# Late rows gathered by two transfers, the first four output tiles stored singly, and 8 KB store runs for three batches, in an attention and spectral-mixing kernel

## The chip, the cores and the metric

The kernel runs on one core of a Trainium2 chip. The time of a run is device microseconds; the number to be compared is the median of several runs. A profiled execution gives, beside its time, the span from the first to the last instruction, every instruction with its line, and every DMA packet.

Names used below: PE is TensorE (matrix products, into PSUM), DVE is VectorE, ACT is ScalarE, POOL is GpSimd, SP is SyncE. SP and POOL each issue DMA transfers here, SP by its hardware queue (q1), POOL by its software queue (q0).

## What is computed

The reference, cut to what matters (batch B = 8, 8 heads, S = 576, head width 64, D = 512, 64 modes):

```
phi(x) = where(x > 0, x, exp(x) - 1) + 1
kv  = einsum('bhsd,bhse->bhde', phi(k), v);  z = sum_s phi(k)
x   = einsum('bhsd,bhde->bhse', phi(q), kv) / (phi(q) . z + 1e-6)     # heads side by side: (8, 576, 512)
X   = rfft(x, axis=1)[:, :64]
Y   = X @ (w_r + i w_i)          # its own 512 x 512 complex matrix for each of the 64 modes
u   = x + irfft(Y, n=576)
out = u + max(u @ w_ch, 0)       # (8, 576, 512) float32
```

The 64 modes' weights (two 512 x 512 float32 matrices each) are most of the bytes read; the output is 9.44 MB.

## The kernel before

**Stages.** Attention, the forward transform, and then one mode after the other: `w_load` (L110) brings a mode's two weight matrices in 512 KB transfers from POOL's queue, `mode_product` (L349 to L365) multiplies, and the mode's rows for all batches are collected in `YT`. Everything that the output needs and that does not depend on the last modes is worked off between the products of the modes, from a list called `work`: the attention rows, the inverse transform of modes 0 to 31 added to x (`fold`, L538), the channel product of that sum (`channel_product`, L557, kept in `E0`), and, for each batch, the rows of modes 32 to 63, as `YZ[b]`.

**YZ.** `YZ[b]` holds in [128 partitions, 2, 512] float16 the 64 rows (32 modes, real and imaginary) twice, in partitions 0 to 63 and 64 to 127, once as they are (index 0, `form_y`, L593) and once multiplied by w_ch (index 1, `form_z`, L584). When it is formed, the last NL = 8 modes are not there yet; their 16 rows (partitions 48 to 63 and 112 to 127) are filled in at the end from the tile `last`, which has the 16 rows of every batch in 128 partitions, row r of batch b in partition 8 r + b.

**The tail** starts when the last weights have landed. PE transposes the late rows (L750), ACT copies them to `last[:, 0]` (L751), PE multiplies them by w_ch in two halves of 256 columns (L757), and ACT and DVE copy a half each to `last[:, 1]` (L763, L765). Tile 0 gets its y part by a product of its own (`y0`, L767, L768). Then 14 transfers from POOL (L771) carry the late rows into the `YZ[b]`, for batches in the order 2, 3, 0, 1, 4, 5, 6, 7; the upper halves of batches 0 and 1 are not needed and left out. The tiles of batches 0 and 1 (pairs 0 to 3) do not wait for these, since they multiply by `last` itself with the selector matrices `lead_sb`.

**Output tiles and pairs.** The output goes out in 36 tiles of [128, 512] float32 (256 KB): four of each batch in `x_main[b]` and, for every two batches, one of the left-over rows in `x_tail`. `pairs` puts them in 18 pairs: 0 and 1 are batch 0, 2 and 3 batch 1, 4 and 5 batch 2, pair 6 and 8 batch 3 with 7 the first two tail tiles, 9 and 10 batch 4, 11 and 12 batch 5, 13 and 14 batch 6, 15 and 17 batch 7 with 16 the other tail tiles. For every pair, all of it pinned in program order on its engine:

- `channels(n)` (L655): PE puts the kept channel product into the pair's two PSUM banks;
- `rectified(n)` (L616, L665): PE adds the late modes' part of the channel product, and ACT takes the max with 0 in place, one tile at a time;
- `finish(n)` (L616, L695): PE adds the late modes' part of u, DVE adds x to the whole pair (128 x 1024) and writes it into x, and SP stores it (`store`, L671, 4 KB runs for two tiles that lie side by side; L677 for tail tiles, 2 KB runs). The last pair is added and stored in single tiles (L690).

PSUM holds four pairs at once. The order on PE at the start of the tail is written by hand at the end of the kernel (L781 to L799): pair 0 in single tiles, then channels(2), channels(3), rectified(2), finish(1), rectified(3), finish(2), and from pair 4 on a loop of channels(n), rectified(n), finish(n - 1). Several transfers of SP can be outstanding; the stores of a queue follow each other.

Of the kernel before, what the change touches and what calls it, by code (L numbers as in the profile page):

```python
# [10 lines left out]
F32 = mybir.dt.float32  # L11
F16 = mybir.dt.float16
BF16 = mybir.dt.bfloat16
AF = mybir.ActivationFunctionType
ALU = mybir.AluOpType
# [27 lines left out]
def kernel(  # L43
# [10 lines left out]
    nc = tc.nc  # L54

    B, H, S, Dh = q.shape
    D = H * Dh
    NM = moe_w_r.shape[0]
    NHP = H // 2
    NDC = D // 128  # L60
    NJJ = 4
# [16 lines left out]
    id16 = const.tile([128, 128], F16, name="id16")  # L78
    fwd_sb = const.tile([128, 5, 2 * NM], F16, name="fwd_sb")
    pick_sb = const.tile([128, 16], F16, name="pick_sb")  # L80
    wch16 = const.tile([128, NDC, D], F16, name="wch16")
# [41 lines left out]
    pin = tc.keep_in_program_order  # L123
# [10 lines left out]
    def rows_of(jj: int, base: int = 0):  # L134

        if jj < NJJ:
            return slice(base + jj, base + 512, NJJ)
        return slice(512, S) if base == 0 else slice(0, base)
# [274 lines left out]
    psW = tc.alloc_tile_pool(name="psW", bufs=1, space=PSUM, side="left")  # L413
# [7 lines left out]
    N_LEAD = 2  # L421
# [31 lines left out]
    sW = ctx.enter_context(tc.tile_pool(name="sW", bufs=1))  # L453
# [1 line left out]
    x_tail = [  # L455
        sW.tile([128, 2, D], F32, tag="x_tail", bufs=B // 4, name=f"x_tail{i}") for i in range(B // 4)
    ]
    YZ = [sW.tile([128, 2, D], F16, tag="YZ", bufs=B, name=f"YZ{b}") for b in range(B)]
    YE: dict[int, object] = {}
    E0: dict[int, object] = {}  # L460
    BASE = (0, 64)
# [2 lines left out]
    def x_of(t: int):  # L464
        if t < B * NJJ:
            return x_main[t // NJJ][:, t % NJJ, :]
        i = t - B * NJJ
        return x_tail[i // 2][:, i % 2, :]
# [13 lines left out]
    last_ps = []  # L482
# [7 lines left out]
    def parts_of(t: int):  # L490
        if t < B * NJJ:
            b, jj = divmod(t, NJJ)
            return [(b, jj, slice(0, 128))]
        p = t - B * NJJ
        return [(2 * p + h, NJJ, HALVES[h]) for h in range(2)]
# [76 lines left out]
    def form_z(b: int):  # L572

        z_ps = bank(f"z{b}")
        for ec in range(NDC):
            yt = YT[:, ec, NF:NM, :].rearrange("p m (t b) -> p (m t) b", b=B)[:, :, b]
            for h in range(2):
# [5 lines left out]
                )  # L583
        pin(nc.scalar.copy(out=YZ[b][:, 1, :], in_=z_ps))  # L584

    def form_y(b: int):

        y_ps = bank(f"yp{b}", [128, NDC, 128], F16)
        for ec in range(NDC):
            yt = YT[:, ec, NF:NM, :].rearrange("p m (t b) -> p (m t) b", b=B)[:, :, b]  # L590
            for h in range(2):
                pin(nc.tensor.transpose(y_ps[HALVES[h], ec, :], yt, id16))
        pin(nc.vector.tensor_copy(out=YZ[b][:, 0, :], in_=y_ps.rearrange("p c r -> p (c r)")))  # L593

    def fold_lead(t: int):
# [4 lines left out]
        sel_rows = inv2_sb[0 : 2 * NF, rows_of(jj, BASE[b % 2])]  # L600
        pin(nc.tensor.matmul(acc, sel_rows, YZ[b][0 : 2 * NF, 0, :]))
        pin(nc.vector.tensor_tensor(out=x, in0=acc, in1=x, op=ALU.add))
        e = E0[b][:, jj * D : jj * D + D]
        acc = bank(f"zb{t}")
        pin(nc.tensor.matmul(acc, id16, e, start=True, stop=False))
        pin(nc.tensor.matmul(acc, sel_rows, YZ[b][0 : 2 * NF, 1, :], start=False, stop=True))
        pin(nc.scalar.copy(out=e, in_=acc))

    last = sW.tile([128, 2, D], F16, tag="rows", bufs=1, name="last")

    def add_inverse(n: int, half: int, tiles_of=(0, 1)):

        def mm(i, orow, l, r):
            on_bank(
                n, {i},
                nc.tensor.matmul(  # L616
                    accs[n][orow, i], l, r, start=False, stop=True, skip_group_check=True
                ),
            )

        for i in tiles_of:
            for b, jj, orow in parts_of(pairs[n][i]):
                sel_rows = rows_of(jj, BASE[b % 2])
                if n < 2 * N_LEAD:
                    mm(i, orow, lead_sb[b][:, sel_rows], last[:, half, :])
                else:
                    g = HALVES[i]
                    mm(i, orow, inv2_sb[g, sel_rows], YZ[b][g, half, :])

    pairs = []  # L630
# [9 lines left out]
    def on_bank(n: int, banks: set, ins):  # L640
        pin(ins)
        for other, theirs in users.setdefault(n, []):
            if not banks & theirs:
                tc.declare_no_dep(ins.ins, other.ins, reason="the other bank of the pair")
        users[n].append((ins, banks))
    accs: dict[int, object] = {}

    def channels(n: int):
        pool = acc_pools[n % 4 // 2]
        accs[n] = pool.tile([128, 2, D], F32, tag="acc", bufs=2, name=f"acc{n}")  # L650
        for i, t in enumerate(pairs[n]):
            for cols, src in e0_parts(t):
                on_bank(
                    n, {i},
                    nc.tensor.matmul(  # L655
                        accs[n][:, i, cols], id16, src, start=(cols.start == 0), stop=False,
                        skip_group_check=True,
                    ),
                )

    def rectified(n: int):
        add_inverse(n, 1)
        for i in range(2):
            a = accs[n][:, i]
            on_bank(n, {i}, nc.scalar.activation(out=a, in_=a, func=AF.Relu))  # L665

    def store(t: int, n_t: int):
        if t < B * NJJ:
            b, jj = divmod(t, NJJ)
            r0 = b * S + BASE[b % 2]  # L670
            nc.sync.dma_start(  # L671
                out=out_rows[r0 : r0 + 512, :].rearrange("(r j) d -> r j d", j=NJJ)[:, jj : jj + n_t, :],
                in_=x_main[b][:, jj : jj + n_t, :],
            )
            return
        i = t - B * NJJ
        nc.sync.dma_start(  # L677
            out=out_rows.rearrange("(i r) d -> r i d", i=B // 2)[512:640, i : i + 2, :],
            in_=x_tail[i // 2],
        )  # L680

    def finish(n: int):
        acc = accs[n]
        single = n == len(pairs) - 1
        t0 = pairs[n][0]
        add_inverse(n, 0)
        for i, t in enumerate(pairs[n]):
            if single:
                x = x_of(t)
                on_bank(n, {i}, nc.vector.tensor_tensor(out=x, in0=acc[:, i], in1=x, op=ALU.add))  # L690
                store(t, 1)
        if single:
            return
        x = x_main[t0 // NJJ][:, t0 % NJJ : t0 % NJJ + 2, :] if t0 < B * NJJ else x_tail[(t0 - B * NJJ) // 2]
        on_bank(n, {0, 1}, nc.vector.tensor_tensor(out=x, in0=acc, in1=x, op=ALU.add))  # L695
        store(t0, 2)

    def spread(n_items: int, step: int, steps: int):
# [43 lines left out]
                work.append(lambda n=n: channels(n))  # L742


    last_ps.append(psW.tile([128, D], F32, tag="P", bufs=2, name="zl1"))
    y_ps = psW.tile([128, NDC, 128], F16, tag="P", bufs=2, name="ypl")
    y0_ps = psW.tile([128, NDC, 8, 2 * B], F32, tag="yt", bufs=1, name="y0l")
    rows = [YT[:, ec, NE:NM, :].rearrange("p m n -> p (m n)") for ec in range(NDC)]
    for ec in range(NDC):
        pin(nc.tensor.transpose(y_ps[:, ec, :], rows[ec], id16))  # L750
    pin(nc.scalar.copy(out=last[:, 0, :], in_=y_ps.rearrange("p c r -> p (c r)")))  # L751
    hw = D // 2
    for h in range(2):
        cols = slice(h * hw, h * hw + hw)
        for ec in range(NDC):
            pin(
                nc.tensor.matmul(  # L757
                    last_ps[h][:, 0:hw], rows[ec], wch16[:, ec, cols],
                    start=(ec == 0), stop=(ec == NDC - 1),
                )  # L760
            )
        if h == 0:
            pin(nc.scalar.copy(out=last[:, 1, cols], in_=last_ps[h][:, 0:hw]))  # L763
        else:
            pin(nc.vector.tensor_copy(out=last[:, 1, cols], in_=last_ps[h][:, 0:hw]))  # L765
    y0 = y0_ps.rearrange("p c m n -> p (c m n)")
    pin(nc.tensor.matmul(y0, lead_sb[0][:, rows_of(0)], last[:, 0, :]))  # L767
    pin(nc.vector.tensor_tensor(out=x_of(0), in0=y0, in1=x_of(0), op=ALU.add))  # L768
    for b in (2, 3, 0, 1, 4, 5, 6, 7):
        for h in range(1 if b < N_LEAD else 2):  # L770
            nc.gpsimd.dma_start(out=YZ[b][64 * h + 48 : 64 * h + 64, :, :], in_=last[b::B, :, :])  # L771
    psW.release()
    acc_pools.append(
        tc.alloc_tile_pool(name="psT1", bufs=1, space=PSUM, side="left", reuse_waits="tile")
# [2 lines left out]
    def relu(n: int, i: int):  # L777
        a = accs[n][:, i]
        on_bank(n, {i}, nc.scalar.activation(out=a, in_=a, func=AF.Relu))

    add_inverse(0, 1)  # L781
    on_bank(
# [2 lines left out]
            out=x_of(0), in0=accs[0][:, 0], scalar=0.0, in1=x_of(0), op0=ALU.max, op1=ALU.add  # L785
        ),
    )
    store(0, 1)
    relu(0, 1)
    rectified(1)  # L790
    channels(2)
    add_inverse(0, 0, (1,))
    on_bank(0, {1}, nc.vector.tensor_tensor(out=x_of(1), in0=accs[0][:, 1], in1=x_of(1), op=ALU.add))
    store(1, 1)
    channels(3)
    rectified(2)
    finish(1)
    rectified(3)
    finish(2)  # L799
    for n in range(4, len(pairs)):  # L800
        channels(n)
        rectified(n)
        finish(n - 1)
# [32 lines left out]
```

## Time and profile before

| What | us |
|---|---|
| median of 4 runs (lowest, highest) | 429.46 (429.01, 430.01) |
| the profiled execution | 429.1 |
| its span, first to last instruction | 427.3 |
| PE busy | 283.9 (66% of the span) |
| DVE busy | 212.3 (50%) |
| ACT busy | 153.5 (36%) |
| POOL busy | 95.6 (22%) |
| software queue (q0): 82.26 MB | 99.0% of the engines' span |
| hardware queue (q1): 9.78 MB | 6.0% |

How to read the views that follow. In the 40 slices each digit is the busy share of a fortieth of the span in tenths, and the GB/s row is what the DMA engines moved in it. The chain of waits gives, for each piece, its start and length in us, the engine, the tile and the line. In the stretches a line has the stretch, its length, then the busy time of PE, PE's weight loads, DVE, ACT and POOL with the number of instructions, then the granted clock of PE, the share of the DMA engines and their GB/s. A row of DMA issues has the transfer, the queue, the number, KB of each, and the median us from issue to landing. A row of DMA queues has packets, MB, and the share of the 16 engines.

### The profile page before, as it was taken

To read this page: it belongs to the slowest core of one execution; us is meant where nothing else is said; L and a number is where in the kernel's file an instruction comes from. 1 tells how busy PE (TensorE), PEld (TensorE's weight loads), DVE (VectorE), ACT (ScalarE), POOL (GpSimd) and SP (SyncE) were. 2 spreads that over 40 slices of the span, in tenths; PEclk is the share of its full clock that TensorE was granted. 3 is DMA by queue.
4 is the path that set the end of the run, shared out by engine and by line. 5 is a ranking of instruction groups with operands and counts; after the bars stand their busy time and mean duration, and the time that the engine had idled before them with its cause. 6 is when DMAs were issued, how large, how long until landed. Compare 5 with 4: busy or idle time off the path is not lost.

```text
span 427.3 us, 6617 instructions
## 1 busy us (share of the span) xinstructions
PE 283.9 (66%) x2692; PEld 158.6 (37%) x2692; DVE 212.3 (50%) x432; ACT 153.5 (36%) x240; POOL 95.6 (22%) x173
## 2 busy tenths in 40 slices
PE   0358777787119665655333797877788778997991
PEld 0346555564004433333111333433334334573320
DVE  1699998956003755556100433434353344421892
ACT  3687666631102100000000244434344343430791
POOL 4232223212201322122122122121121112010600
PEclk9996666656557655555555569899898899999996
DMA  8999999999999999999999999999999999996697
GB/s 150 207 208 209 209 210 209 212 214 212 220 211 214 214 214 213 215 212 214 214 214 212 213 214 214 213 214 213 214 214 212 214 214 214 213 214 133 221 406 301
DMA packets 35854, 92.46 MB, mean 216 GB/s; under 512 B 3216, under 2 KB 16400, under 8 KB 35824
## 3 DMA queue, kind: packets, MB, share of 16 engines
q0 software_dynamic: 32256, 82.26, 99.0%
q1 hardware_dynamic: 3568, 9.78, 6.0%
q8 instruction: 21, 0.34, 0.3%
q14 instruction: 9, 0.07, 0.0%
HBM read 163.93 MB, written 9.44 MB: 406 GB/s over the span
## 4 chain that ended last, share of the span: by engine, by line
DMA 77%; PE 8%; DVE 6%; issue 5%; POOL 1%; ACT 1%; DVEq 0%; POOLq 0%
DMA wi<-in_moe_w_i_dram 61%; DMA wr<-in_moe_w_r_dram 4%; DMA pick_sb<-row_pick 4%; DMA q<-in_q_dram 4%; DMA k<-in_k_dram 3%; PE acc L616 3%; PE P L349 2%; DVE x L267 2%; PE acc L655 2%; DVE qe L195 1%; ACT ke L182 1%; DVE q L189 1%; DVE rd L264 0%; ACT qT L218 0%; DVE k L189 0%
## 5 line engine op out<-in xcount | busy, mean ns | idle before, releaser
L349 PE MATMUL P<-wi,xt_c 128*32 128x512 bf16 x252 | 37.4, 530 | 42.4 <-DMA wi<-in_moe_w_i_dram 42.4
L360 ACT CAST ys<-P 128x512 f16<-128x512 f32 x31 | 18.1, 585 | 125.9 <-PE P L349 125.9
L110 POOL DMA_DIRECT2D wr<-in_moe_w_r_dram x64 | 34.0, 531 | 123.1 <-PE P L349 101.2
L110 POOL DMA_DIRECT2D wi<-in_moe_w_i_dram x65 | 34.5, 531 | 117.2 <-PE P L349 89.3
L358 DVE CAST ys<-P 128x512 f16<-128x512 f32 x32 | 22.1, 690 | 72.7 <-PE P L349 72.7
L349 PEld LDWEIGHTS <-xt_c 128*32 128x32 bf16 x504 | 28.6, 155 | 77.2 <-issue 65.9
L349 PE MATMUL P<-wr,xt_c 128*32 128x512 bf16 x252 | 37.8, 539 | 21.2 <-DMA wr<-in_moe_w_r_dram 19.3
L557 PE MATMUL eps<-wch,xTw 128*128 128x512 f16 x144 | 42.1, 421 | 0.0
L538 DVE TENSOR_TENSOR x_main<-ya,x_main 128x512 f32<-128x512 f32 x32 | 22.1, 691 | 40.0 <-PE ya L534 39.9
L146 PEld LDWEIGHTS <-qT 64*128 64x128 f16 (+1 forms) x640 | 23.5, 126 | 41.4 <-issue 21.3
L365 PE MATMUL yt<-pick_sb,ys 128*128 128x16 f16 x252 | 16.5, 175 | 25.4 <-DMA pick_sb<-row_pick 15.1
L540 ACT CAST x16w<-x_main 128x512 f16<-128x512 f32 x32 | 19.8, 618 | 34.5 <-DVE x_main L538 34.5
L565 ACT CAST E<-eps 128x512 f16<-128x512 f32 (+1 forms) x40 | 21.3, 543 | 27.0 <-PE eps L557 27.0
L146 PE MATMUL num<-kv,qT 64*128 64x65 f16 (+1 forms) x320 | 13.6, 225 | 22.9 <-ACT kv L242 19.5
L365 PEld LDWEIGHTS <-ys 128*128 128x128 f16 x252 | 12.1, 102 | 40.6 <-issue 17.8
L182 ACT ACTIVATE qe<-q 128x1152 f16<-128x1152 f16 x16 | 17.7, 1156 | 22.8 <-DMA q<-in_q_dram 22.8
L211 PE MATMUL qTp<-id,qe 128*128 128x128 f16 x144 | 16.7, 311 | 11.8 <-DVE qe L195 11.4
L267 DVE TENSOR_TENSOR x<-num,rd 128x512 f16<-128x512 f32 x32 | 22.1, 692 | 1.1
L146 PE MATMUL nw<-kv,qT 64*128 64x65 f16 (+1 forms) x320 | 19.6, 236 | 1.1 <-DVE x_tail L508 0.9
L182 ACT ACTIVATE ke<-k 128x1152 f16<-128x1152 f16 x16 | 17.7, 1155 | 4.9 <-DMA k<-in_k_dram 4.9
L211 PEld LDWEIGHTS <-qe 128*128 128x128 f16 x144 | 14.7, 147 | 12.6 <-DVE qe L195 11.4
L665 ACT ACTIVATE acc<-acc 128x512 f32<-128x512 f32 x34 | 18.1, 581 | 2.3 <-PE acc L616 1.7
(101 smaller groups left out, 449.4 us busy)
## 6 DMA issues: line engine op xcount, KB each, us to landing
wr<-in_moe_w_r_dram POOLq DMA_DIRECT2D x64, 512.0 KB, 18.7
wi<-in_moe_w_i_dram POOLq DMA_DIRECT2D x63, 512.0 KB, 18.9
out_dram<-x_main SPq DMA_DIRECT2D x14, 512.0 KB, 5.8
q<-in_q_dram POOLq DMA_DIRECT2D x8, 576.0 KB, 13.3
k<-in_k_dram POOLq DMA_DIRECT2D x8, 576.0 KB, 14.4
v<-in_v_dram POOLq DMA_DIRECT2D x8, 576.0 KB, 16.6
out_dram<-x_main SPq DMA_DIRECT2D x4, 256.0 KB, 3.7
out_dram<-x_tail SPq DMA_DIRECT2D x2, 512.0 KB, 6.2
```

Source lines behind the costliest of these rows:

```text
L110: tc.keep_in_program_order(nc.gpsimd.dma_start(out=w[:, dcs], in_=rows_of[:, dcs, :]))
L146: mm = nc.tensor.matmul(num[hpo][orow, c0 : c0 + 65], qT[rows, hpp, h2, cols], kv_sb[rows, hpp, h2, :])
L182: pin(nc.scalar.activation(out=ev[:, c], in_=heads(nm, b)[:, c], func=AF.Exp))
L211: nc.tensor.transpose(qT_ps[:, j].rearrange("p t r -> p (t r)"), phi["q", b][:, hpp, j].rearrange("p o d -> p (o d)"), id16,)
L267: nc.vector.tensor_tensor(out=dst.rearrange("p (o c d) -> p o c d", o=2, c=4), in0=nv[:, :, :, 0:64], in1=rden.unsqueeze(3).broadcast_to([ ...
L349: nc.tensor.matmul(P[dc * 32 : dc * 32 + 32, :], xt_cols(dc, t, kk), w[:, dc, :], start=(t == 1), stop=(t == 0), tile_position=(0, dc * 32),)
L358: fixed(nc.vector.tensor_copy(out=st, in_=P))
L365: nc.tensor.matmul(yt_ps[:, ec, kk % 8, :], st[:, ec * 128 : ec * 128 + 128], pick_sb)
L538: pin(nc.vector.tensor_tensor(out=x, in0=acc, in1=x, op=ALU.add))
L540: pin(nc.scalar.copy(out=x16w[t], in_=x))
L557: nc.tensor.matmul(e_ps, xT[:, c, :], wch16[:, c, :], start=(c == 0), stop=(c == NDC - 1))
L565: pin(nc.scalar.copy(out=dst, in_=e_ps[:, cols]))
```

## The change

- `YZ` becomes one tile `YZ_all` [128, 8, 2, 512], of which `YZ[b]` is a slice.
- The 14 gathers become two, one for each half of the partitions, 16 partitions x 8 batches x 2 KB each; the lower half is issued by SP, ahead of the first store, the upper half by POOL.
- The transposed late rows go through two PSUM tiles, one copied by ACT and one by DVE; both halves of the product by w_ch are copied by ACT. The PSUM tiles of this stage change places (`z1` takes the slot of `y0`, and `y0` one of the two slots of the transposes).
- Pair 1 is finished in two single tiles, as pair 0 is, and on PE `channels(3)` moves from ahead of `rectified(2)` to behind pair 1.
- For batches 4, 5 and 6 a pair's add issues no store of its own; the second pair's add issues one store of all four tiles (1 MB, 8 KB runs in the output).

```
-    YZ = [sW.tile([128, 2, D], F16, tag="YZ", bufs=B, name=f"YZ{b}") for b in range(B)]
+    YZ_all = sW.tile([128, B, 2, D], F16, tag="YZ", bufs=1, name="YZ_all")
+    YZ = [YZ_all[:, b] for b in range(B)]
...
+    QUADS = (4, 5, 6)
...
         on_bank(n, {0, 1}, nc.vector.tensor_tensor(out=x, in0=acc, in1=x, op=ALU.add))
+        if t0 < B * NJJ and t0 // NJJ in QUADS:
+            if t0 % NJJ:
+                store(t0 - 2, NJJ)
+            return
         store(t0, 2)
...
-    last_ps.append(psW.tile([128, D], F32, tag="P", bufs=2, name="zl1"))
-    y_ps = psW.tile([128, NDC, 128], F16, tag="P", bufs=2, name="ypl")
-    y0_ps = psW.tile([128, NDC, 8, 2 * B], F32, tag="yt", bufs=1, name="y0l")
+    z1_ps = psW.tile([128, NDC, 8, 2 * B], F32, tag="yt", bufs=1, name="z1l")
+    y_ps = [
+        psW.tile([128, NDC, 128], F16, tag="P", bufs=2, name=f"ypl{h}")[:, 0 : NDC // 2] for h in range(2)
+    ]
+    y0 = psW.tile([128, D], F32, tag="P", bufs=2, name="y0l")
+    last_ps.append(z1_ps.rearrange("p c m n -> p (c m n)"))
...
-        pin(nc.tensor.transpose(y_ps[:, ec, :], rows[ec], id16))
-    pin(nc.scalar.copy(out=last[:, 0, :], in_=y_ps.rearrange("p c r -> p (c r)")))
+        pin(nc.tensor.transpose(y_ps[ec // 2][:, ec % 2, :], rows[ec], id16))
+    pin(nc.scalar.copy(out=last[:, 0, COLS[0]], in_=y_ps[0].rearrange("p c r -> p (c r)")))
+    pin(nc.vector.tensor_copy(out=last[:, 0, COLS[1]], in_=y_ps[1].rearrange("p c r -> p (c r)")))
...
-        if h == 0:
-            pin(nc.scalar.copy(out=last[:, 1, cols], in_=last_ps[h][:, 0:hw]))
-        else:
-            pin(nc.vector.tensor_copy(out=last[:, 1, cols], in_=last_ps[h][:, 0:hw]))
+        pin(nc.scalar.copy(out=last[:, 1, COLS[h]], in_=last_ps[h][:, 0:hw]))
...
-    for b in (2, 3, 0, 1, 4, 5, 6, 7):
-        for h in range(1 if b < N_LEAD else 2):
-            nc.gpsimd.dma_start(out=YZ[b][64 * h + 48 : 64 * h + 64, :, :], in_=last[b::B, :, :])
+    for h, eng in enumerate((nc.sync, nc.gpsimd)):
+        eng.dma_start(
+            out=YZ_all[64 * h + 48 : 64 * h + 64].rearrange("r b z d -> r b (z d)"),
+            in_=last.rearrange("p z d -> p (z d)"),
+        )
...
+    def add_one(n: int, i: int):
+        t = pairs[n][i]
+        on_bank(n, {i}, nc.vector.tensor_tensor(out=x_of(t), in0=accs[n][:, i], in1=x_of(t), op=ALU.add))
+        store(t, 1)
...
     channels(2)
     add_inverse(0, 0, (1,))
-    on_bank(0, {1}, nc.vector.tensor_tensor(out=x_of(1), in0=accs[0][:, 1], in1=x_of(1), op=ALU.add))
-    store(1, 1)
+    add_one(0, 1)
+    rectified(2)
+    for i in range(2):
+        add_inverse(1, 0, (i,))
+        add_one(1, i)
     channels(3)
-    rectified(2)
-    finish(1)
     rectified(3)
     finish(2)
```

More of the change, by code (lines that the diff above doesn't have):

```diff
@@ L742 @@
                 work.append(lambda n=n: channels(n))
-    last_ps.append(psW.tile([128, D], F32, tag="P", bufs=2, name="zl1"))
-    y_ps = psW.tile([128, NDC, 128], F16, tag="P", bufs=2, name="ypl")
-    y0_ps = psW.tile([128, NDC, 8, 2 * B], F32, tag="yt", bufs=1, name="y0l")
+    z1_ps = psW.tile([128, NDC, 8, 2 * B], F32, tag="yt", bufs=1, name="z1l")
[4 more added lines that the diff above has]
+    last_ps.append(z1_ps.rearrange("p c m n -> p (c m n)"))
     rows = [YT[:, ec, NE:NM, :].rearrange("p m n -> p (m n)") for ec in range(NDC)]
+    hw = D // 2
+    COLS = [slice(h * hw, h * hw + hw) for h in range(2)]
     for ec in range(NDC):
-        pin(nc.tensor.transpose(y_ps[:, ec, :], rows[ec], id16))
-    pin(nc.scalar.copy(out=last[:, 0, :], in_=y_ps.rearrange("p c r -> p (c r)")))
-    hw = D // 2
+        pin(nc.tensor.transpose(y_ps[ec // 2][:, ec % 2, :], rows[ec], id16))
+    pin(nc.scalar.copy(out=last[:, 0, COLS[0]], in_=y_ps[0].rearrange("p c r -> p (c r)")))
+    pin(nc.vector.tensor_copy(out=last[:, 0, COLS[1]], in_=y_ps[1].rearrange("p c r -> p (c r)")))
     for h in range(2):
-        cols = slice(h * hw, h * hw + hw)
         for ec in range(NDC):
@@ L757 @@
                 nc.tensor.matmul(
-                    last_ps[h][:, 0:hw], rows[ec], wch16[:, ec, cols],
+                    last_ps[h][:, 0:hw], rows[ec], wch16[:, ec, COLS[h]],
                     start=(ec == 0), stop=(ec == NDC - 1),
@@ L761 @@
             )
-        if h == 0:
-            pin(nc.scalar.copy(out=last[:, 1, cols], in_=last_ps[h][:, 0:hw]))
-        else:
-            pin(nc.vector.tensor_copy(out=last[:, 1, cols], in_=last_ps[h][:, 0:hw]))
-    y0 = y0_ps.rearrange("p c m n -> p (c m n)")
+        pin(nc.scalar.copy(out=last[:, 1, COLS[h]], in_=last_ps[h][:, 0:hw]))
     pin(nc.tensor.matmul(y0, lead_sb[0][:, rows_of(0)], last[:, 0, :]))
     pin(nc.vector.tensor_tensor(out=x_of(0), in0=y0, in1=x_of(0), op=ALU.add))
-    for b in (2, 3, 0, 1, 4, 5, 6, 7):
-        for h in range(1 if b < N_LEAD else 2):
-            nc.gpsimd.dma_start(out=YZ[b][64 * h + 48 : 64 * h + 64, :, :], in_=last[b::B, :, :])
+    for h, eng in enumerate((nc.sync, nc.gpsimd)):
[3 more added lines that the diff above has]
+        )
     psW.release()
```

## The prediction

> **What bounds the kernel now.** I read the 40 slices of the page first, then the chain of waits of the last 33 us, then busy time and DMA by stretches, then the DMA issues and the timelines of SP, POOL, PE and DVE.
>
> ```profile
> PE   0358777787119665655333797877788778997991
> DVE  1699998956003755556100433434353344421892
> DMA  8999999999999999999999999999999999996697
> GB/s 150 207 208 209 209 210 209 212 214 212 220 211 214 214 214 213 215 212 214 214 214 212 213 214 214 213 214 213 214 214 212 214 214 214 213 214 133 221 406 301
> ```
>
> Up to slice 36 the DMA engines are full with the weights and no compute engine is. The change leaves that stage alone, but for where the rows of YZ lie. It acts in the last four slices: the last weight lands, the transfers stop, and the output (9.44 MB) has to go out. The chain of waits of this tail, after the last mode:
>
> ```profile
> 394.47 0.40 PE ypl L750 x4
> 394.87 0.89 PE zl L757 x8
> 395.78 0.43 DVE last L765
> 396.26 1.05 PE acc L616 x4
> ...
> 417.27 1.23 DVE x_tail L695
> 418.50 0.60 DVEq L831
> 419.09 0.60 DVE x_main L690
> ```
>
> It names PE and DVE, but ends with the add at 419.7, and the span lasts to 427.3. The 7.6 us behind it are stores still on their way. So I take the transfers themselves by stretches (last two columns: share of the DMA engines, GB/s):
>
> ```profile
> 398.50:400.00 1.50, 1.50 (x8) 0.74 (x7) 0.90 (x2) 1.32 (x4) 1.50 (x4) 1.00 0.89 313
> 400.00:401.50 1.50, 1.50 (x8) 0.55 (x7) 1.50 (x2) 1.25 (x3) 1.50 (x4) 1.00 0.61 205
> 401.50:403.00 1.50, 1.50 (x11) 0.27 (x8) 1.50 (x3) 1.24 (x4) 1.50 (x5) 1.00 0.95 343
> 403.00:404.50 1.50, 1.50 (x13) 0.56 (x12) 1.50 (x2) 1.48 (x3) 0.47 (x1) 1.00 0.97 346
> 404.50:406.00 1.50, 1.50 (x14) 0.48 (x10) 1.47 (x2) 1.11 (x4) 0.00 (x0) 1.00 0.95 341
> 406.00:422.00 16.00, 11.89 (x66) 2.92 (x63) 13.47 (x13) 10.68 (x20) 0.00 (x0) 0.92 1.02 405
> 422.00:424.00 2.00, 0.00 (x0) 0.00 (x0) 0.00 (x0) 0.00 (x0) 0.00 (x0) 0.50 1.03 389
> ```
>
> From 406 to 424 the engines are full at 405 GB/s (389 in 2 KB runs). The store stream sets the end, DVE runs ahead of it (one pair of tiles, 524 KB, in 1.13 to 1.25 us of DVE and 1.29 us of DMA), and SP's issues stretch from 0.33 us at 400.56 to 1.91 at 411.16. **What counts is how many store bytes are out by 406.** Up to there the stream is poor: it moved 1.5 x (313+205+343+346+341) = 2322 KB where 405 GB/s would be 3037, and part of that was gathers:
>
> ```profile
> YZ<-last POOLq DMA_DIRECT2D x14, 32.0 KB, 2.8
> ```
>
> POOL issues them from 396.78 to 403.47. Two stream before 398.5 (a window from 397.8 to 398.45 shows 0.06 MB of the software queue); 12 x 32 KB = 384 KB come later. Stores out by 406: 2322 - 384 = 1938 KB.
>
> **The change, part by part.** *The late rows.* The second half of z is copied by ACT (L763 row: 0.38) and no longer by DVE (L765: 0.42), ready at 396.16 for 396.20; ACT is idle there until 396.97, so this costs nothing. The y copy is halved between ACT and DVE; neither is late, as the y0 product (395.58) waits for PE's eight z products in front of it anyway. DVE loses L765, so the y0 add moves from 396.12 to about 396.0. I give the tail 0.1 us from this (bounds 0.05 and 0.2).
>
> *Tiles 2 and 3 singly.* Before, the pair add starts at 399.31 after 0.60 us of waiting for PE, and its store is issued at 400.56. Now channels(3) (two products of 0.22 on PE) stands behind, so rectified(2) runs at 397.8 and the product for tile 2 at 398.2; ACT's relu of it is done at 398.04. DVE adds tile 2 when tile 1 is done: 398.6 to 399.3, tile 3 to 400.0 (0.69 each; two cost 1.38 for 1.23). Stores at 399.3 and 400.0, half a pair 1.2 us and the other half 0.5 us earlier. PE then has channels(3), rectified(3) and finish(2), six products of 0.22 from 398.9: the add of pair 2 starts at 400.3 (was 400.45), its store is issued at 401.55 (was 401.69). So this part moves two tiles only; behind them DVE's own pace rules, 0.13 us ahead.
>
> *Fourteen gathers become two*, of 256 KB each (512 KB, as the unused upper halves of batches 0 and 1 go along). POOL loses 6.69 us of issuing, and nobody but the gathers waited for POOL. SP issues one at about 396.2, ahead of store(0) on its queue; SP is idle until 397.63. POOL's goes out at about 396.7 (it needed 0.58 us after the data before, too). With the 0.87 us that store(0) takes from issue (397.63) to stream (398.50), the first flows at 397.1, with POOL's 1.0 us (issue 396.78, first bytes about 397.85) the second at 397.8: in the empty stretch ahead of the stores. The trace shows no such transfer. Bounds: at the stream's 405 GB/s 0.65 us each; the slowest burst that I find where gathers lie back to back is
>
> ```profile
> q0 software_dynamic: 96, 0.10, 43.3%
> ```
>
> in the window 400.3 to 401.0, 98 KB in about 0.66 us, or 149 GB/s: 1.76 us each. I take 1.1. Landing takes 0.5 to 1.1 us more (the 32 KB ones land 1.8 at least, 2.8 median, after issue). So both are in the rows between 399.1 and 401.7; taken: 400.2.
>
> The wait that this adds: rectified(4) on PE reads both transfers' rows (every batch under one count), where before it needed only the first two gathers. PE reaches it at 400.5. Behind it on PE stand the two products of finish(3), for which DVE waits, and then a store. Pair 3's bytes are due when pair 2's are out (402.4 + 1.29); with 0.87 of issue, 1.2 of adding and 0.9 of PE work this allows a landing up to about 400.65. Later than that costs one for one.
>
> [...]
>
> *What the stream then does.* Tiles 0 to 3 (1049 KB) flow from 398.4, each as its store comes, until 401.5; pair 2 starts at 402.4. From there the supply holds; at the share that the stretches from 401.5 show (0.96), 3.6 us x 405 x 0.96 = 1400 KB by 406. Stores out by 406: 2449 KB, 511 more than before: **1.26 us**.
>
> *8 KB runs* for batches 4 to 6 (3.15 MB). Per packet, 2 KB at 389 GB/s is 84 ns and 4 KB at 405 is 162, so a packet carries some 6 ns of its own; 8 KB would be 413 GB/s: a gain of 0.16 us, or 0 if the runs are cut at 4 KB. Taken: 0.08. Against it, the first pair of a batch waits 1.15 us for the second. Pairs 2 to 8 are out at 411.6; batch 4's store is issued at 411.0 and flows at 411.9: 0.3 us dry for most engines. But one engine has the window's instruction fetch to carry ("q8 instruction: 1, 0.02, 0.5%" from 410 to 423, 1.0 us on one of 16), ends last and is never dry. Taken: 0.1 (bounds 0 and 0.4). Tiles 2 and 3 in 2 KB runs: 0.05.
>
> Sum: -1.26 - 0.08 + 0.1 + 0.05 = -1.2 us. The profiled execution took 429.1 (span 427.3 and 1.8 around it), so 427.9; it lies 0.36 under the median of the runs, 429.46, so on that scale **428.3**.
>
> **Rivals.** *B, the gain is eaten by the gathers (no change).* All bytes of both go to the same engines in series, store(0) queues behind the first on SP's ring, and both run at 149 GB/s: 397.1 + 2 x 1.76 = 400.6, in the rows at 401.7, pair 3 1.05 us late, and the four singles shoved to 403.3. For it: 16 rows only, and large. Against: the halves go to different partitions, and most of the gathers' packets show no longer time than the stores'. Gain 0.1 to 0.2: 429.3.
>
> *C, slower.* The same wait at rectified(4), with a landing beyond 400.65 + 1.26 = 401.9; that is where two transfers in series run under 137 GB/s. The farthest row is the fourteen gathers' own mean, 448 KB in 6.69 us, 67 GB/s (set by POOL's issuing): 3.9 us each, landing at 405.9, 4 us slower on balance. At two thirds of the burst's rate, 100 GB/s, it would be 403.3 and 1.4 us slower: 430.9. For it: one count for all batches, so the batch needed first waits for the last. Against: the burst.
>
> *D, the change does not do what it says*: YZ as one tile makes copies and products of the form stage (L584, L593, L601) wait for each other, or SP issues store(0) first. The first is hidden by the weights (the chain there is 18.7 us pieces of wi), and x_main's halves are already added and stored without waits within one tile. Price about the whole gain: 429.4.
>
> **How the numbers follow.** About 0.2% (0.86 us) is what a measurement can tell from no change. Forecast 0.60, of which 0.52 faster (under 428.6) and 0.08 within; B 0.22 (0.04 faster, 0.16 within, 0.02 slower); C 0.14, all slower; D 0.04 within. Faster 0.56, within 0.28, slower 0.16. The forecast's own range is 427.6 to 428.9 (gathers at 0.65 us each, nothing dry, up to a landing of 401.2). Reaching over B and the near part of C: 427.6 to 430.2.
>
> **What would show it.** Right: two gathers that flow before 399.5; four 256 KB stores with the fourth issued near 400.0; no wait for a transfer at L616; share 0.9 or more from 402.4 on; the last add of DVE barely earlier, the last landing 1.2 us earlier. Wrong: PE idle in front of rectified(4) until after 400.7 with DVE idle behind it (B, C); a share under 0.9 near 411.6 (the 8 KB stores); any wait by L584 or L593 that grows between 358 and 383 (D).

## The result, and the profile after

The changed kernel takes 430.2 us (median of 43 runs, 429.03 to 432.17) where the kernel before takes 429.24 (64 runs): **0.21% slower, ratio 1.0021, 95% interval 1.0012 to 1.003**. The forecast was 1.2 us faster. Its profiled execution took 430.15 us, with a span of 428.4.

The two executions differ by 1.05 us, which falls in two parts. I count the tail from the end of DVE's copy of the last mode's rows (L402): 394.41 before, 394.95 after. From there to the end of the span it is 32.92 us before and 33.42 after, **0.5 us longer**. The other 0.54 us lies ahead of the tail, and the last part of this text comes back to it.

In the chain of waits of the changed kernel's tail (start, length, what) a transfer stands where before only PE and DVE stood:

```profile
396.98 5.99 DMA YZ_all<-last
402.97 0.04 issue
403.01 0.93 PE acc L617 x3
```

POOL's gather is issued at 396.98 and lands at 402.97. The DMA issues between 396.5 and 403.2 (number, KB of each, us to landing):

```profile
out_dram<-x_main SPq DMA_DIRECT2D x4, 256.0 KB, 4.9
out_dram<-x_main SPq DMA_DIRECT2D x1, 512.0 KB, 4.6
YZ_all<-last SPq DMA_DIRECT2D x1, 256.0 KB, 5.4
YZ_all<-last POOLq DMA_DIRECT2D x1, 256.0 KB, 6.0
```

A 32 KB gather had taken 2.8 us. These take 5.4 and 6.0, and the single stores beside them 4.9 where the first one before took 2.5. PE in program order, with the wait in brackets:

```profile
400.54 0.59 PE L656 MATMUL acc<-E,id 128*128 128x512 f16 x2
402.18 0.37 PE L617 MATMUL acc<-YZ_all,inv_sb 64*128 64x512 f16 x1 [1.04 <-DMA YZ_all<-last]
403.01 0.37 PE L617 MATMUL acc<-YZ_all,inv_sb 64*128 64x512 f16 x1 [0.47 <-DMA YZ_all<-last]
```

These are channels(4) and the two products of rectified(4): the lower tile waits for SP's gather, the upper one for POOL's. The products of finish(3) stand behind them, and DVE waits for those:

```profile
403.98 2.36 DVE L698 TENSOR_TENSOR x_main<-acc,x_main 128x1024 f32<-128x1024 f32 x2 [2.02 <-PE acc L617]
```

The stretches (last two columns: share of the DMA engines, GB/s):

```profile
398.50:400.00 1.50, 1.50 (x8) 0.73 (x7) 1.50 (x3) 1.46 (x3) 0.00 (x0) 1.00 1.13 187
400.00:401.50 1.50, 1.14 (x6) 0.43 (x5) 1.16 (x2) 1.07 (x2) 0.00 (x0) 1.00 1.01 134
401.50:403.00 1.50, 0.37 (x1) 0.11 (x1) 0.47 (x1) 0.41 (x1) 0.00 (x0) 1.00 0.98 280
403.00:404.50 1.50, 1.49 (x7) 0.49 (x8) 0.52 (x1) 0.75 (x2) 0.00 (x0) 1.00 1.07 412
404.50:406.00 1.50, 1.50 (x10) 0.26 (x6) 1.50 (x2) 1.23 (x3) 0.00 (x0) 1.00 0.80 326
...
413.00:415.00 2.00, 2.00 (x12) 0.37 (x8) 2.00 (x3) 1.74 (x5) 0.00 (x0) 1.00 0.78 305
```

The first two lines are the ones to learn from. The DMA engines are *full* (share 1.13 and 1.01) and move 187 and 134 GB/s, against 405 where they carry stores: they are held, not idle. At 404.5 they are short of work (0.80), since DVE is 2 us late. At 413 they are short again (0.78): the first 1 MB store, of batch 4, is issued at 413.56 and its first packet runs at 414.40.

### The profile page after: what moved, and what is told of

Read it like the earlier page. It is cut to its first block, busy times and chain, and to the rows that moved or that the text cites. A ratio compares the mean times of both kernels' runs of the same rounds, so it can differ in the third digit from the quotient of the medians.

```text
span 428.4 us, 6605 instructions
## 1 busy us (share of the span) xinstructions
PE 283.8 (66%) x2692; PEld 159.0 (37%) x2692; DVE 212.7 (50%) x433; ACT 153.9 (36%) x241; POOL 89.3 (21%) x160
## 4 chain that ended last, share of the span: by engine, by line
DMA 74%; PE 11%; DVE 6%; issue 5%; POOL 1%; ACT 1%; DVEq 0%; POOLq 0%
DMA wi<-in_moe_w_i_dram 61%; DMA pick_sb<-row_pick 4%; DMA q<-in_q_dram 4%; DMA k<-in_k_dram 3%; PE P L349 3%; PE acc L617 2%; DVE x L267 2%; PE acc L656 1%; DMA YZ_all<-last 1%; PE z L580 1%; PE zb L607 1%; PE zb L606 1%; PE yb L602 1%; DVE qe L195 1%; ACT ke L182 1%
```

## The experiments

The theory (L): the two large gathers land too late, PE's products for pair 4 wait for them, and the stores behind run late; without that, the change gains. Rivals: Q, the 1 MB stores starve the stream; D, YZ as one tile makes the form stage wait.

All results first. Times are us from the copy L402 of each profiled execution; the ratio is that of the runs to the kernel before on the same chip.

| kernel | large gathers landed | PE waits at pair 4 | last store landed | ratio (95%) |
|---|---|---|---|---|
| before | (14 small) | 0 | 31.93 | 1 |
| changed | 7.18, 8.02 | 1.51 | 32.38 | 1.0021 (1.0012 to 1.003) |
| after14 | (14 small) | 0 | 31.09 | 0.9994 (0.9982 to 1.0007) |
| two_only | 6.33, 8.31 | 1.61 | 32.53 | 1.0040 (1.0027 to 1.0052) |
| noquad | 6.84, 8.24 | 1.73 | 32.76 | 1.0032 (1.002 to 1.0044) |
| h0_only | 6.02 | 0 | 30.52 | single run |
| yz_tile | (14 small) | 0 | 32.08 | 0.9997 (0.9987 to 1.0007) |
| best14 | (14 small) | 0 | 31.04 | 0.9989 (0.9976 to 1.0002) |
| mix14 | (14 small) | 0 | 31.44 | 0.9987 (0.997 to 1.0004) |
| singles | (14 small) | 0 | 31.72 | 0.9995 (0.9973 to 1.0017) |
| quad_only | (14 small) | 0 | 31.55 | 0.9995 (0.9977 to 1.0014) |
| one_half | (8 small) | 0 | 34.00 | 1.0061 (1.004 to 1.0083) |
| spread_rows | 4.98, 5.89 | 0 | 30.38 | **0.9966 (0.9953 to 0.998)** |
| pool_both | 6.28, 8.34 | 1.69 | 32.71 | single run |

**after14: the change with the old gathers.**

```
-    for h, eng in enumerate((nc.sync, nc.gpsimd)):
-        eng.dma_start(out=YZ_all[64 * h + 48 : 64 * h + 64]..., in_=last...)
+    for b in (2, 3, 0, 1, 4, 5, 6, 7):
+        for h in range(1 if b < N_LEAD else 2):
+            nc.gpsimd.dma_start(out=YZ[b][64 * h + 48 : 64 * h + 64, :, :], in_=last[b::B, :, :])
```

> The changed kernel with the fourteen gathers of before from POOL; all else of the change kept. Theory L (late landing: the two large gathers landed at 402.1 and 403.0, PE stood 1.0 and 0.5 us in front of rectified(4), DVE 2.0 us behind it): with small gathers the wait goes, DVE has no gap over 0.4 us between 399 and 405, and the kernel is 0.6 to 1.4 us faster than the changed one, so 0.2% to no change against before (ratio 0.998 to 1.000; the gathers again lie beside the stores, which takes back most of the 1.26 us that was forecast). Rival Q (the loss comes from the 1 MB stores of batches 4 to 6 and not from the landing): DVE's gap goes, but the time stays within 0.3 us of the changed kernel, ratio 1.001 to 1.003.

The wait is gone, the tail is 1.2 us shorter than the changed kernel's, and the ratio falls from 1.0021 to 0.9994, a time that can't be told from before. Its stretches, from 3.6 us after the copy (same columns):

```profile
397.70:399.20 1.50, 1.50 (x8) 0.73 (x7) 1.50 (x3) 1.44 (x3) 1.50 (x4) 1.00 0.73 239
399.20:400.70 1.50, 1.50 (x9) 0.54 (x7) 1.16 (x2) 1.08 (x3) 1.50 (x4) 1.00 0.87 286
400.70:402.20 1.50, 1.50 (x9) 0.45 (x9) 1.40 (x2) 1.24 (x3) 1.50 (x4) 1.00 0.96 329
```

No stretch here is held as the changed kernel's were. Theory L passes, Q fails: the 1 MB stores are still in this kernel.

**two_only: the large gathers alone, in the kernel before** (YZ as one tile, the two transfers of the change, nothing else).

> The kernel before with the two large gathers (and YZ as one tile) alone; order of the tail, copies of the late rows and stores as before. Theory L: both land 5 to 6 us after issue, near 402 to 403, PE waits 1.5 to 2.4 us at the product for pair 4 that it reached at 400.6, and the kernel is 0.6 to 1.6 us slower than before, ratio 1.0015 to 1.004. Rival Q: the gathers alone cost nothing or gain, ratio 0.997 to 1.000.

1.7 us slower by the ratio. PE:

```profile
401.13 0.37 PE L617 MATMUL acc<-YZ_all,inv_sb 64*128 64x512 f16 x1
403.12 0.37 PE L617 MATMUL acc<-YZ_all,inv_sb 64*128 64x512 f16 x1 [1.61 <-DMA YZ_all<-last]
```

The lower gather is just in time here (it landed 4.5 us after issue, earlier than the 5 to 6 expected), the upper one 1.6 us late. By the medians this edit alone costs more than the whole change, so that the other edits would give part of it back; the two intervals overlap, so this is likely and not shown.

**noquad: the change with two-tile stores** (`QUADS = ()`).

> The changed kernel with two-tile stores for batches 4 to 6, as before. In the changed kernel the store stream runs at 0.53 to 0.75 of the DMA engines from 413.5 to 415, after batch 4's first pair waited for its second. If that costs the end: 0.3 to 0.5 us faster than the changed kernel, ratio to before 1.000 to 1.0015. If the late landing alone counts: within 0.2 us of the changed kernel, ratio 1.0015 to 1.003. Under rival Q alone: back at before or better, ratio 0.997 to 1.000.

Slower than the change, if anything, so the short share at 413 in the changed kernel is not where the time goes. The shortage itself did go,

```profile
413.00:415.00 2.00, 2.00 (x12) 0.48 (x12) 2.00 (x3) 1.85 (x4) 0.00 (x0) 1.00 0.99 389
```

but my expectation that this would save 0.3 to 0.5 us was wrong: the last store lands 0.4 us later than the change's (32.76 for 32.38), the second gather 0.2 later. Why the time gained did not show is open.

**quad_only: the 1 MB stores alone, in the kernel before.**

> The kernel before with the 1 MB stores for batches 4 to 6 alone. If 8 KB runs are really cheaper per byte (8 KB packets took 300 to 330 ns in the changed kernel, two of 4 KB 325): 0 to 0.3 us faster, ratio 0.9993 to 1.000. If the stream runs dry while the second pair is awaited: a stretch under 0.9 of the DMA engines near 411 to 414 and ratio 1.000 to 1.001.

Between 1.0 us faster and 0.6 slower by the interval, so not settled by time; in the profile the stream never runs dry (0.98 or more in each microsecond from 410 to 416) and carries more:

```profile
405.00:411.00 6.00, 6.00 (x33) 1.41 (x32) 5.91 (x6) 5.36 (x11) 0.00 (x0) 1.00 1.02 404
...
413.00:420.00 7.00, 4.72 (x28) 1.35 (x26) 6.39 (x7) 4.28 (x8) 0.00 (x0) 1.00 1.01 413
```

404 GB/s with mostly 4 KB runs, 413 with mostly 8 KB.

**singles: the early single tiles alone, in the kernel before.**

> The kernel before with tiles 2 and 3 added and stored singly and channels(3) behind them on PE; gathers, copies of the late rows and stores of later batches as before. If the early tiles give what the prediction gave them apart from the gathers (two tiles 0.5 to 1.2 us earlier, the rest 0.13 us): 0.2 to 0.5 us faster, ratio 0.999 to 0.9995. If DVE's extra 0.15 us counts more: 1.000 to 1.0005.

Tiles 2 and 3 are stored 4.97 and 5.57 us after the copy (the pair: 6.15) and the last store lands 0.2 us earlier. The ratio is 0.9995 with too wide an interval to say more.

**yz_tile: only YZ as one tile, in the kernel before.**

> The kernel before with YZ as one tile of eight slices and nothing else changed. Rival D of the prediction (one tile makes the copies and products of the form stage wait for each other): waits of ACT and DVE between 355 and 384 grow, the last weights land later, ratio 1.001 to 1.002. Against it: no change, ratio 0.999 to 1.001.

No change. The waits of the form stage (engine, line, what it waited for: us, times, longest) are, with one tile,

```profile
DVE YZ_all L594 <- PE yp L593: 10.2, 7, 2.0
```

and the same to the digit in the kernel before:

```profile
DVE YZ L593 <- PE yp L592: 10.2, 7, 2.0
```

ACT's (8.4 us, 8 times, longest 1.6) are the same in both, too. D falls.

**h0_only: SP's gather alone; the upper halves' late rows are left out.**

> The changed kernel with SP's gather (lower partitions) alone; the upper halves of the late rows are left out. It shows how long one such transfer takes by itself. If the two transfers share one limit (together 512 KB in 4.95 us, 106 GB/s, from the first packet at 398.02 to the second landing at 402.97), it lands 3.9 to 4.6 us after issue (5.4 with both). If each has a limit of its own, it lands at 5.2 to 5.6 as before. If bytes alone count, as for a 256 KB store (2.5), it lands at 2.5 to 3.2. PE's wait at rectified(4) shrinks by as much as the landing comes earlier.

```profile
YZ_all<-last SPq DMA_DIRECT2D x1, 256.0 KB, 4.3
```

4.3 us alone and 5.4 with its twin; no wait at PE. So the two delay each other, but even one is far over the 2.5 of a 256 KB store.

**micro: transfers of 256 KB one at a time.** Zeros are stored as the output; then each transfer waits for the one before.

> Not the kernel's computation: zeros are stored as the output and then transfers of 256 KB inside SBUF run one at a time, two rounds, 2 KB runs, from 128 partitions to: 16 neighbouring partitions (d16), 32 (d32), 64 (d64), 128 (d128), 16 partitions eight apart (dstep), all from SP; 16 from POOL (dpool); SP and POOL together into the lower and upper 16 (dlo, dhi) and into the same 16 (dlo, dsame); eight of 32 KB from POOL (dsmall). If what counts is how few places of SBUF the destination reaches: d16 3.8 to 4.5 us from issue to landing, d128 2.2 to 2.8, d32 and dstep between them. [...] If bytes alone count: all 2.2 to 2.8. For the pair: if the engines work off one transfer after the other, dlo and dhi land as late as dlo and dsame (the second 6 to 6.5 us after issue); if the two halves of SBUF take data side by side, dlo and dhi are clearly earlier than dlo and dsame.

(The profile leaves the numbers out of names: `d` is d16, d32, d64 and d128.)

```profile
d<-src SPq DMA_DIRECT2D x8, 256.0 KB, 3.9
dlo<-src SPq DMA_DIRECT2D x4, 256.0 KB, 4.5
dstep<-src SPq DMA_DIRECT2D x2, 256.0 KB, 3.0
dpool<-src POOLq DMA_DIRECT2D x2, 256.0 KB, 4.1
dhi<-src POOLq DMA_DIRECT2D x2, 256.0 KB, 6.1
dsame<-src POOLq DMA_DIRECT2D x2, 256.0 KB, 6.3
```

In the second round d16, d32, d64 and d128 took 4.1, 3.9, 3.9 and 2.3. The bytes and the runs are the same, so the place decides. Much of the difference lies behind the packets: d16's run for 1.6 us, from 1.2 to 2.8 after issue, and it lands 1.3 us later; d128's run for 0.8 and it lands 0.3 later. Of the pair, the second lands at 6.1 into the other half of SBUF and at 6.3 into the same 16 partitions: going to the other half gains 0.2 us, and they are 2.0 and 2.2 us behind the 4.1 of one alone.

**micro_spread: the same with other places.**

> As the earlier run of transfers one at a time (zeros as output, not the kernel's computation), 256 KB from SP each, now to: 16 neighbouring partitions (dnext), 16 four apart within the lower half (dfour), 16 eight apart over both halves (deight), 32 neighbours across the middle (dacross, 48 to 79), 32 four apart (dboth), 64 across the middle (dmid, 32 to 95), every second partition (dtwo), all (dall); then 16 four apart in the upper half (dupper), and dfour and dupper together from SP and POOL. Before: 16, 32 and 64 neighbours in the lower half 4.1, 3.9 and 3.9 us, 16 eight apart 3.0, 128 2.3. If the half of SBUF is the limit: dfour 3.9 to 4.1, all that reach both halves 2.2 to 3.1. If neighbours are the limit: dfour near 3.0, dacross near 4.0.

```profile
dfour<-src SPq DMA_DIRECT2D x4, 256.0 KB, 3.1
dnext<-src SPq DMA_DIRECT2D x2, 256.0 KB, 4.4
deight<-src SPq DMA_DIRECT2D x2, 256.0 KB, 3.0
dacross<-src SPq DMA_DIRECT2D x2, 256.0 KB, 3.9
dboth<-src SPq DMA_DIRECT2D x2, 256.0 KB, 2.3
dmid<-src SPq DMA_DIRECT2D x2, 256.0 KB, 2.8
dtwo<-src SPq DMA_DIRECT2D x2, 256.0 KB, 2.4
dall<-src SPq DMA_DIRECT2D x2, 256.0 KB, 2.3
dupper<-src SPq DMA_DIRECT2D x2, 256.0 KB, 3.0
dupper<-src POOLq DMA_DIRECT2D x2, 256.0 KB, 3.9
```

Sixteen partitions four apart take 3.0 in one half alone, where sixteen neighbours took 4.1, and 32 neighbours across the middle are as slow (3.9) as within a half: here the neighbourhood counts and not the half. But 64 neighbours take 2.8 across the middle (dmid) and took 3.9 within one half (d64), so the half counts too, and neither alone orders all the rows. The pair of spread transfers (dfour and dupper's POOL row) lands at 3.1 and 3.9, where the neighbours landed at 4.5 and 6.1. (dnext's median holds a first transfer behind the zero stores, 4.6; the other took 4.1.)

**spread_rows: the change with the late rows at every fourth partition.** The order of YZ's rows is free as long as the selector has the same one. The rows of modes 32 to 55 are kept in a tile `Y2` whose every fourth place stays empty, the last modes in `YL`; the transfers have the same number, bytes and runs, and the same work is computed.

```
-        ...tensor_copy(out=sel[:, 0, h * 64 : h * 64 + 64], in_=id16[:, 2 * NF : 128])
+        ...tensor_copy(out=sel[:, 0, h * 64 : h * 64 + 64].rearrange("p (s c) -> p s c", c=4),
+                       in_=id16[:, 2 * NF : 128].rearrange("p (c s) -> p s c", c=4))
...
+    Y2 = ystage.tile([128, NDC, 16, 4, B], F16, name="Y2")
...
-            out=YZ_all[64 * h + 48 : 64 * h + 64].rearrange("r b z d -> r b (z d)"),
+            out=YZ_all[64 * h + 3 : 64 * h + 64 : 4].rearrange("r b z d -> r b (z d)"),
```

> The changed kernel with the late rows at every fourth partition of each half of YZ (3, 7, ... 63 and 67 ... 127) and no longer at 48 to 63 and 112 to 127; the rows of the selector and of the early modes change places with them, so the same is computed, by the same two transfers of the same bytes. If neighbouring destination partitions are what made the transfers late: they land 3.1 to 3.5 us (SP) and 3.8 to 4.5 us (POOL) after issue where it was 5.4 and 6.0, PE's wait in front of rectified(4) falls from 1.5 us to under 0.5, and the gain that the prediction looked for appears: last landing 0.8 to 1.6 us earlier than before (counted from the copy of the last mode's rows), ratio 0.996 to 0.999. If the length of the transfers or their running in series beside the stores is the cause: landing and time as in the changed kernel, ratio 1.001 to 1.004.

```profile
out_dram<-x_main SPq DMA_DIRECT2D x4, 256.0 KB, 3.1
out_dram<-x_main SPq DMA_DIRECT2D x1, 512.0 KB, 2.8
YZ_all<-last SPq DMA_DIRECT2D x1, 256.0 KB, 3.2
YZ_all<-last POOLq DMA_DIRECT2D x1, 256.0 KB, 3.9
```

3.2 and 3.9 us to landing, as in the run by itself; single stores 3.1 for 4.9; no wait at PE. POOL's 64 data packets took 202 ns each on average, 480 in the changed kernel. The stretches (the copy ends at 395.01, so they can be laid on those of the changed kernel):

```profile
398.50:400.00 1.50, 1.50 (x8) 0.69 (x7) 1.48 (x3) 1.50 (x4) 0.00 (x0) 1.00 1.06 315
400.00:401.50 1.50, 1.50 (x9) 0.53 (x8) 1.16 (x2) 1.08 (x3) 0.00 (x0) 1.00 0.98 337
401.50:403.00 1.50, 1.50 (x10) 0.45 (x8) 1.39 (x2) 1.18 (x3) 0.00 (x0) 1.00 0.95 361
```

315, 337 and 361 GB/s for 187, 134 and 280. The kernel is **1.5 us faster than before** (ratio 0.9966) and beats both kernels. Nothing of the change was taken away, only the place of the rows. The edit also keeps the rows in other tiles ahead of the tail, but the gain is in the tail itself, counted from the copy: 31.42 us for 33.42. So the place was the cause.

**pool_both: both large gathers from POOL**, so that none stands ahead of the stores on SP's queue.

> The changed kernel with both large gathers issued by POOL, so that none stands ahead of the stores on SP's ring. If the first store's delay (landed 5.4 us after issue, 2.5 before) comes from standing behind the gather on the same ring: it lands 2.5 to 3.5 us after issue, while the second gather lands about 0.5 us later than the 8.0 of the changed kernel (from the copy of the last rows). If the engines themselves are held by the gathers, the first store still takes 4 us or more.

The first store, with no gather ahead of it on its queue now, still lands 5.4 us after issue (3.10 to 8.53 after the copy), and the second gather 0.3 us later than in the change. From 398.8 to 401.6 the DMA engines move 149 GB/s on average here too. The engines are held, not the queue.

**best14, mix14, one_half: other ways to get the rows there.** best14 is after14 with eight YZ tiles; mix14 issues the lower gathers of batches 2, 3 and 4 from SP; one_half sends only the eight lower gathers and reads the lower copy for both tiles (`g = HALVES[0]`).

> The changed kernel with the fourteen gathers and the eight YZ tiles of before; the single tiles, the copies of the late rows and the 1 MB stores of the change stay. The same tail as with one tile and fourteen gathers (last landing 0.84 us earlier than before, counted from the copy of the last mode's rows): ratio 0.997 to 0.9995, and within 0.1% of the run with one tile if the tile does nothing, 0.1 to 0.2% better if rival D holds.

> As the one before, with the lower gathers of batches 2, 3 and 4 issued by SP ahead of its first store (0.35 us each) and the other eleven by POOL. Three gathers less lie beside the stores and POOL is done 1.4 us earlier: last landing 0.1 to 0.4 us earlier than with all from POOL, ratio 0.996 to 0.999. If SP's three push the first store back by more than they save: within 0.1% of it or slower.

> The run with fourteen gathers and eight YZ tiles, but only the eight lower gathers: both tiles of a pair multiply by the lower copy of the rows, so 192 KB less lie beside the stores. The DMA engines get 0.4 to 0.6 us back. Against it, two products of 64 rows can't run side by side on PE any more (0.33 us for two, 0.43 one after the other): some 0.2 us more for a pair of tiles, 1.3 to 1.4 us for each, where the store stream needs 1.29. If the stream still sets the end: ratio 0.997 to 0.999; if PE becomes the bound: DVE gets gaps of 0.1 to 0.2 us in front of each pair and the ratio is 1.000 to 1.005.

best14 and mix14 lie between 0.3% faster and no change. mix14's earlier gathers were expected to land the last store 0.1 to 0.4 us earlier than best14's; it landed 0.4 later in the one profile, and the ratios do not differ. In one_half PE becomes the bound, as its second branch had it: two products of 64 rows no longer overlap (four take 1.05 us at 403.33, where the kernel before had 0.62 at 401.90 and 0.84 at 402.99), and DVE waits for PE twelve times, 3.6 us in all. The gaps are 0.3 us where 0.1 to 0.2 were expected, and the ratio lies above that branch's 1.005: one_half is 2.6 us slower.

## Why the prediction was wrong

- *What bounds the tail*: right, but for one_half, where PE does. What counts is how many store bytes are out by 406 on the scale of before, 11.6 us after the copy. The rows of the hardware queue up to there, in before (396.30 to 406.00), changed (396.84 to 406.54) and spread_rows (396.90 to 406.60):

```profile
q1 hardware_dynamic: 665, 1.94, 54.0%
q1 hardware_dynamic: 912, 2.03, 66.7%
q1 hardware_dynamic: 1119, 2.81, 79.7%
```

  Less SP's gather (0.26 MB) this is 1.94, 1.77 and 2.55 MB of stores; the forecast was 2.45. At 405 GB/s the changed kernel is 0.4 us behind and spread_rows 1.5 ahead, and their last stores land 0.45 later and 1.55 earlier.
- *The copies of the late rows*: right in size. The last of them ends 1.74 us after the copy L402 (1.79 before), the y0 add starts 0.12 us earlier.
- *Tiles 2 and 3 singly*: right. Stores were forecast at 399.3, 400.0 and 401.55 on the scale of before, that is 4.9, 5.6 and 7.1 us after the copy, and came at 4.88, 5.48 and 7.04.
- **The fourteen gathers become two: the step that failed.** The sum let the first flow from 397.1, took 1.1 us for each (0.65 to 1.76) and 0.9 to the landing: 400.2, or 5.8 us after the copy. They landed at 7.18 and 8.02. On the scale of before, the packets of the two ran from 397.5 to 401.0, and the second landed at 402.4. POOL's packets were all under way by then (window 397.9 to 401.6 of the changed kernel's own time):

```profile
q0 software_dynamic: 80, 0.26, 52.8%
```

  Of the 2.2 us between 400.2 and 402.4, 0.4 is the later start, 1.35 the flow (3.55 us for 2.2) and 0.5 the landing (1.4 us behind the last packet, where 0.5 to 1.1 was allowed). The flow is 512 KB at 148 GB/s, the rate of the burst that was the slow end of the range: the row was right, and the 1.1 that I took lay between it and the stream's full rate, where no row stood. What the burst did not show is how long such transfers take from the last packet to the landing; with that, 512 KB took 4.95 us (398.02 to 402.97), 106 GB/s. The landing I allowed came from the 32 KB gathers. That gathers hold the stores beside them stood in rival B and not in the sum: the four single stores landed 8.46 to 10.41 us after the copy, in spread_rows 6.71 to 8.62.
- *The wait that this adds*: right in place (rectified(4)), near in limit and price. The landing was 1.8 us beyond the limit of 400.65; against spread_rows, whose landing (5.89) is within it, the tail is 2.0 us longer. That 1.8 less the forecast gain of 1.26 is just the 0.5 by which the tail is longer than before is partly luck, since the gain without the wait was 1.5. This is rival C, held too unlikely (0.14) by the same mis-sized term. B had the flow of 1.76 us each right, but a landing at 401.7.
- *8 KB runs*: right in rate (413 GB/s, as worked out). The dry stretch was right in place and near 0.3 us, though taken at 0.1: in spread_rows, where DVE is not late, batch 4's store is issued 16.7 us after the copy (forecast: 16.6), and just ahead of its first packet (412.54) stands

```profile
412.00:413.00 1.00, 1.00 (x7) 0.26 (x6) 1.00 (x2) 0.85 (x2) 0.00 (x0) 1.00 0.67 266
```

  In quad_only and after14, whose streams are behind, nothing runs dry there (share 0.98 or more from 410 to 416 in quad_only, 1.04 from 405.2 to 412.2 in after14).
- *D*: its first half is refuted by yz_tile (the 18.7 us piece of the chain that stands over the form stage is of wr, not of wi); of its second, SP issued the gather 1.3 us ahead of store(0).
- *The sum*, 1.2 us faster if the gathers land in time: spread_rows, where they do, is 1.5 us faster (0.9 to 2.0).

One thing stays open. The median says 0.9 us (0.5 to 1.3), the tail of the one profiled execution 0.5. A tail repeats to about 0.15 us where no large gather is in it (32.92 in before, 33.06 in yz_tile; 32.19 in after14, 32.14 in best14). With the two gathers into neighbours it was 33.42 in the change, 33.45 in two_only, 33.81 in pool_both and 34.11 in noquad, so the change's own may vary more; this was not tried.

The 0.54 us ahead of the tail show nothing of the change: over the fourteen profiled kernels the copy L402 ended anywhere from 394.0 to 395.7. In the profiled execution of the change PE's granted clock (third from last) was halved for a while,

```profile
370.00:374.00 4.00, 4.00 (x16) 1.36 (x16) 1.39 (x2) 1.17 (x2) 0.00 (x0) 0.50 1.07 215
```

where the kernel before had

```profile
370.00:374.00 4.00, 4.00 (x38) 2.60 (x38) 2.10 (x4) 1.76 (x3) 0.00 (x0) 1.00 1.07 215
```

16 products for 38, and POOL issued the last weight transfers up to 2.2 us later. Only two_only and one_half show the same dip. But in spread_rows and yz_tile, which do not, the copy ended at 395.01 and 395.08, later than the change's 394.95: that the dip cost the 0.54 us is not shown.

## What to carry to other kernels

Price a transfer by where it writes, not only by its bytes: the same 256 KB took 2.3 us into 128 partitions, 3.0 into sixteen four apart and 4.1 into sixteen neighbours, and while it was held it held the stores beside it (single stores landed after 4.9 us beside neighbours, 3.1 beside spread rows). When small transfers are merged, the consumer that needed the first piece waits for the last (1.51 us of PE here), so work out the landing of the whole against the moment of the first use. Where the order of rows is free, choose it for the transfer; here that turned 0.2% slower into 0.3% faster.

## What the runs showed that I had not expected

- Full DMA engines at a third of the rate: share 1.01 at 134 GB/s from 400.0 to 401.5, for 405 with stores. The share alone would have read as saturation.
- Two transfers from two queues into different halves of SBUF end as late as two into the same partitions (6.1 and 6.3 us). Spread over every fourth partition, the second ends at 3.9.
- 32 and 64 neighbouring partitions within one half are hardly faster than 16 (3.9 for 4.1 us), and 64 across the middle take 2.8, while 16 four apart need 3.0 and 32 four apart 2.3. Why neighbours are slow is not shown by these runs.
- The packets of a transfer can be done long before it lands: 1.3 us before into sixteen neighbours, 0.3 into 128 partitions. A rate read from packets alone leaves that out.
